# Block attention and two MLPs on one core: Strassen's products for y and o in the last stage too

## The chip, the core and the metric

The kernel runs on one core of a Trainium2 chip. The core has five engines with queues of their own: TensorE (PE, matrix products; PEld is its loading of weights), VectorE (DVE), ScalarE (ACT), GpSimd (POOL) and SyncE (SP), which issues the DMAs. An engine works off its queue in order and waits on semaphores for the others. The metric is the device time of one execution in microseconds (us).

## The reference

```
scores = q @ k.T / 8            # 4 batches, 8 heads, 576 positions, 64 wide
scores[block(i) < block(j)] = -1e9               # blocks of 64 positions
x = softmax(scores) @ v         # -> x: 2304 tokens x 512
x = (sigmoid(x @ w_gate) * (x @ w_val)) @ w_out  # 512 -> 1536 -> 512
h = x @ w_in                                     # 512 -> 2048
out = max(0.01 * h, h) @ w_out2                  # 2048 -> 512
```

The MLP weights arrive as float64, and all is computed to float32's precision.

## The kernel before

Activations are kept transposed, features on partitions, tokens along the free axis. For precision every operand of a product is split into a high and a low half (`hi_lo`: `copy` L336 makes the high half on ACT or DVE, `sub` L350 the low half on DVE, both recorded at L339/L341 and L352), and a product of a 128 x 128 weight block with 512 columns is three matmuls: high x high, high x low, low x high.

The 2304 tokens go through in three stages: 768, 512 and 1024 tokens. In the first, the weights are converted from float64 and their halves are written to HBM (`wd`); later stages load them from there (`weights`, L913; w tiles: 7 buffers of 512 KB). The attention of the next tokens runs between the products of the first two stages. A stage computes gate and val (12 row blocks each, in three groups of four), y = their product times w_out, then h (16 row blocks in four groups) and o. Here y and o are the names of the two output products, and their units carry a group g and an output row block mo. They are delayed by a group (`late`), so that gate or h products stand between a group's making and its use.

In the last stage (b = 2 and 3 are its two halves of 512 tokens) gate, val and h are made in pairs by Strassen's algorithm (Winograd's form): `pair_unit` (L1079) makes two row blocks for both token halves with seven products, B11, T1, T2, B21, T3, B22, T4, six matmuls each (L1099), where eight would be needed. Its results are C11, C12, C21, C22 (`finish`). The sums of weight blocks that it needs were formed in the middle stage by `sums` (L931: additions at L941 on DVE or POOL, then halves, then stores to `ds`), and the sums of x by `mix` (L1032). y and o of the last stage are plain: `half_unit` (L1184), 12 matmuls (L1209) into a PSUM bank of ring mm, and one DVE addition to the accumulator (L1270; xt, shown as x). Their inputs are the four blocks of a group, split by `split_g`.

A planner sets the order. Every operation is given to `Plan.op` with an engine (or two to choose from), a cost, a due time, what it reads and writes, and the ring buffers it uses; `Plan.order` (L149) plays the program through and hands out each engine's next operation, the due time deciding among those that are ready. The due times come from the list `order` (L828 to L850) and the costs.

Of the kernel before, what the change touches and what calls it, by code (L numbers as in the profile page):

```python
# [8 lines left out]
F32 = mybir.dt.float32  # L9
# [9 lines left out]
P = 128  # L19
# [27 lines left out]
def f32(ap):  # L47
    return ap.bitcast(F32)
# [176 lines left out]
def block_attention_then_two_mlps(  # L225
# [35 lines left out]

    const = pool("const", 1)
# [47 lines left out]
    ds = [dram.tile([P, 2, 8 * P], F32, name=f"ds{i}") for i in range((2 * N1 + N2) // 2)]  # L310
# [517 lines left out]
    LATE = [(2, 0), (3, 0), (2, 1), (3, 1), (2, 2), (2, 3), (3, 2), (3, 3)]  # L828
    again = set()
# [3 lines left out]
    for g in range(N1 // G):  # L833
        ms = range(G * g, G * g + G, 2)
        whole([("gate", 2, m) for m in ms])
        rest = late[6:] if g == N1 // G - 1 else []
        whole(late[:len(late) - len(rest)])
        whole([("val", 2, m) for m in ms])
        whole(rest)
        again.update(rest)  # L840
        late = [("y", b, g, mo) for b, mo in LATE]
    whole([("y", b, g, mo) for mos in ((0, 1), (2, 3)) for b in (2, 3) for mo in mos])
    late = []
    for g in range(N2 // G):
        hs = [("h", 2, m) for m in range(G * g, G * g + G, 2)]
        rest = late[6:] if g == N2 // G - 1 else []
        whole(hs[:1] + late[:len(late) - len(rest)] + hs[1:] + rest)
        again.update(rest)
        late = [("o", b, g, mo) for b, mo in LATE]
# [6 lines left out]
    def paired(u):  # L856
        return u[1] == 2 and u[0] in ("gate", "val", "h")
# [70 lines left out]
    def half_pair(u):  # L928
        return {"gate": 0, "val": N1 // 2, "h": N1}[u[0]] + u[2] // 2

    def sums(u, w0, w1):  # L931
# [18 lines left out]
        a11, a12, a21, a22 = [lambda wf=wf, k=k: wf[:, k * q:(k + 1) * q] for wf in wfs for k in range(2)]  # L950
        s1, s2, s3, s4 = [lambda k=k: s[:, k * q:(k + 1) * q] for k in range(4)]
# [8 lines left out]
    def weights_of_pair(u):  # L960
# [7 lines left out]
        load(ws[1], lambda: f32(ws[1][:, :, q:]), wd[k + 1][:, :, q:], P * 8 * q, d - 13, [("wd", k + 1)], [ws[1]])  # L968
# [63 lines left out]
    def mix(d):  # L1032
# [6 lines left out]
        def two(out, x, y, alu, reads, uses, e):  # L1039
            op(  # L1040
                ("dve", "pool"), (c_dve(n), 0.25 + n / 450),
                lambda eng: engines[eng].tensor_tensor(out[:, :n], x(), y(), alu), reads, [out], uses, e, port=True,
            )
# [11 lines left out]
        for k in range(2):  # L1055
            (y1, a1, u1), (y2, a2, u2), (z1, b1, _), (z2, b2, _) = of(k, 2), of(k + 2, 2), of(k, 3), of(k + 2, 3)
            t1, t2, t3, t4 = [r_gf.tile() for _ in range(4)]
            e = d + 2 + 4 * k
            two(t1, z1, y1, ALU.subtract, [*b1, *a1], [t1, *u1], e)
            two(t2, z2, lambda t1=t1: t1[:, :n], ALU.subtract, [t1, *b2], [t1, t2, *u2], e + 0.5)  # L1060
            part("T2", k, lambda t2=t2: t2[:, :n], [t2], [t2], e + 1)
            two(t3, z2, z1, ALU.subtract, [*b1, *b2], [t3, *u1, *u2], e + 1.5)
            part("T3", k, lambda t3=t3: t3[:, :n], [t3], [t3], e + 2)
            two(t4, y2, lambda t2=t2: t2[:, :n], ALU.subtract, [t2, *a2], [t4, t2, *u2], e + 2.5)
            part("T4", k, lambda t4=t4: t4[:, :n], [t4], [t4], e + 3)
            part("T1", k, lambda t1=t1: t1[:, :n], [t1], [t1], e + 3.5)
            part("B21", k, y2, a2, u2, e + 4)
            part("B22", k, z2, b2, u2, e + 4.5)


    places = {"g": [], "sg": [], "tmp": []}
# [6 lines left out]

    def pair_unit(u, ws):  # L1079

# [7 lines left out]
        cost = 6 * c_mm(n)  # L1088
        q = 2 * P
        t = [0.0]  # L1090

        def product(p, first, w, col, x):
            wt = ws[w]
            srcs = [quarter(x, k) for k in range(2)]

            def f():
                for k in range(2):
                    for wl, xl in ((0, 0), (0, 1), (1, 0)):
                        nc.tensor.matmul(  # L1099
                            p[:, :n], lhsT=wt[:, wl, col + k * P:col + (k + 1) * P], rhs=srcs[k][0][:, xl],  # L1100
# [3 lines left out]
            reads = [wt, *[x for _, toks, _ in srcs for x in toks]]  # L1104
            op(
                "pe", cost, f, reads, [p], [p, wt, *[x for _, _, us in srcs for x in us]], d + t[0],
                slack=0.0 if first else CHAIN,
            )
            t[0] += cost
# [7 lines left out]

        out = {}
        for name, b, j in (("C22", 3, 1), ("C11", 2, 0), ("C12", 3, 0), ("C21", 2, 1)):
            if kind == "gate":  # L1120
                gates[b, m + j] = place("sg")
                view, tok, host = gates[b, m + j]
                out[name] = view, tok, host, b, j
            else:
                key = "y" if kind == "val" else "o", b, m + j
                gf[key] = r_gf.tile()
                view, toks, host = held_g[key] = places["g"].pop(0)
                gt[key], g_toks[key] = view, (toks, host)
                f = gf[key]
                out[name] = (lambda f=f: f[:, :n]), (f, 0), f, b, j  # L1130

        def finish(name, p, x=None):
# [12 lines left out]
            if kind == "gate":  # L1145
                op("act", c_act(n, psum), lambda: nc.scalar.activation(dst(), src(), AF.Sigmoid), reads, [tok], uses, e)
                return
            key = "y" if kind == "val" else "o", b, m + j
            if kind == "h":
# [14 lines left out]
            split_g(key, e + 0.6)  # L1164

        a, c, r = b_sc.tile(), b_tp.tile(), b_mm.tile()
# [247 lines left out]
```

## Time and profile before

| | us |
|---|---|
| median of three runs (1007.94 to 1009.1) | 1008.2 |
| the profiled execution | 1007.89 |
| its span on the core | 1006.1 |
| PE busy | 994.5 |
| DVE busy | 645.9 |
| ACT busy | 509.7 |
| POOL busy | 127.3 |

The busy times are shares of one span, and the engines work side by side, so they don't add up. PE's clock was granted in full in every slice (1.00, 2.4 GHz). The page's chain of waits, followed back from the last instruction, is 98% PE.

### The profile page before, as it was taken

The numbers are of one execution on the slowest core, as the hardware profiler recorded it, in microseconds if no ns is written. First come the engines' busy times: TensorE is split into PE (matmuls) and PEld (weight loads), VectorE is DVE, ScalarE is ACT, GpSimd is POOL, SyncE is SP. The second block draws the span as 40 slices with busy tenths as digits, with TensorE's granted clock in tenths as the row PEclk, the third lists the DMA queues.
The fourth block names the chain that finished last, engine by engine and source line by source line (L and its number), as shares of the span: only waits on it lengthen the run. The fifth ranks groups of instructions, "written<-read, shape, count | busy, mean of one in ns | idle before, by whom it ended". The sixth has DMA issues, their size and how long they took to land.

```text
span 1006.1 us, 15306 instructions
## 1 busy us (share of the span) xinstructions
PE 994.5 (99%) x5552; PEld 796.1 (79%) x5552; DVE 645.9 (64%) x1454; ACT 509.7 (51%) x1041; POOL 127.3 (13%) x144
## 2 busy tenths in 40 slices
PE   7999999999999999999999999999999999999998
PEld 4588888978888878777877778788888878888886
DVE  6989989889989657747577665726033357423432
ACT  7988785676766435464455534343333125431420
POOL 2422000220002002211222011102010110000000
PEclk9999999999999999999999999999999999999999
DMA  7488886856876438778767655565446544543542
GB/s 205 143 292 267 274 263 237 257 186 235 280 249 212 167 122 307 262 237 302 229 214 237 226 194 182 184 217 174 150 146 209 156 138 138 165 146 106 177 136 84
DMA packets 75724, 203.91 MB, mean 203 GB/s; under 512 B 8576, under 2 KB 21376, under 8 KB 75648
## 3 DMA queue, kind: packets, MB, share of 16 engines
q1 hardware_dynamic: 75648, 202.93, 62.1%
q8 instruction: 44, 0.72, 0.3%
q14 instruction: 32, 0.26, 0.1%
HBM read 141.56 MB, written 61.34 MB: 202 GB/s over the span
## 4 chain that ended last, share of the span: by engine, by line
PE 98%; DVE 1%; ACT 0%; DMA 0%; issue 0%; SPq 0%
PE mm L1209 63%; PE sc L1099 11%; PE tp L1099 6%; PE sc L425 3%; PE tp L630 3%; PE mm L1099 3%; PE pa L654 2%; PE tp L425 2%; PE tp L566 1%; PE mm L654 1%; PE tp L581 1%; PE pa L425 1%; DMA qk<-in_qk 0%; PE pa L770 0%; PE sc L727 0%; PE mm L581 0%
## 5 line engine op out<-in xcount | busy, mean ns | idle before, releaser
L1209 PE MATMUL mm<-g,w 128*128 128x512 f32 (+1 forms) x1080 | 240.7, 367 | 0.2 <-DVE g L352 0.2
L1209 PE MATMUL mm<-x,w 128*128 128x512 f32 (+2 forms) x1008 | 236.9, 387 | 0.0
L1209 PEld LDWEIGHTS mm<-g,w 128*128 128x128 f32 x1080 | 184.0, 188 | 36.7 <-issue 2.4
L1209 PEld LDWEIGHTS mm<-x,w 128*128 128x128 f32 x1008 | 179.8, 188 | 40.6 <-issue 5.1
L1099 PE MATMUL sc<-both,w 128*128 128x512 f32 x480 | 119.9, 394 | 0.0
L1099 PEld LDWEIGHTS sc<-both,w 128*128 128x128 f32 x480 | 90.3, 188 | 20.6
L497 ACT ACTIVATE both<-both,nm 128x256 f32<-128x256 f32 (+5 forms) x148 | 84.5, 573 | 31.1 <-DVE nm L482 30.1
L893 ACT ACTIVATE mag<-raw 128x512 f32<-128x512 f32 x68 | 45.7, 672 | 47.0 <-DVE wf L907 17.8
L1209 PE MATMUL mm<-sg,w 128*128 128x512 f32 (+1 forms) x288 | 67.4, 365 | 0.0
L352 DVE TENSOR_TENSOR g<-gf,g 128x512 fp32r<-128x512 f32 (+2 forms) x74 | 55.5, 752 | 14.2 <-ACT g L339 14.0
L1270 DVE TENSOR_TENSOR x<-mm,x 128x512 f32<-128x512 f32 x40 | 27.6, 691 | 57.3 <-PE mm L1209 57.2
L907 POOL TENSOR_TENSOR wf<-mag,rnd 128x512 int32<-128x512 int32 x28 | 37.3, 1334 | 206.1 <-DVE w L352 150.2
L1209 PE MATMUL mm<-xa,w 128*128 128x256 f32 x480 | 62.7, 281 | 0.0
L1209 PEld LDWEIGHTS mm<-xa,w 128*128 128x128 f32 x480 | 60.0, 188 | 3.3 <-issue 0.8
L517 POOL TENSOR_SCALAR both<-both,r 128x256 f32<-128x256 f32 (+6 forms) x61 | 36.2, 601 | 183.4 <-DVE r L510 153.8
L1209 PEld LDWEIGHTS mm<-sg,w 128*128 128x128 f32 x288 | 49.9, 188 | 9.4
L482 DVE CUSTOM_DVE_ANT_0 both<-sc,mask 128x256 f32<-128x256 f32 (+6 forms) x101 | 39.3, 424 | 19.4 <-PE sc L425 19.3
L1270 DVE TENSOR_TENSOR acc<-mm,acc 128x512 f32<-128x512 f32 (+1 forms) x60 | 36.0, 600 | 22.9 <-PE mm L1209 22.2
L515 ACT ACTIVATE both<-both,r 128x512 f32<-128x512 f32 (+6 forms) x87 | 45.1, 564 | 8.7 <-DVE r L510 8.6
L901 DVE SCALAR_TENSOR_TENSOR mag<-raw,mag 128x512 int32<-128x512 int32 x68 | 47.5, 700 | 0.3
L425 PE MATMUL sc<-qk 64*128 64x384 f32 (+5 forms) x228 | 42.2, 421 | 5.4 <-DMA qk<-in_qk 5.4
L352 DVE TENSOR_TENSOR w<-wf,w 128x512 fp32r<-128x512 f32 x68 | 46.9, 689 | 0.2
(177 smaller groups left out, 1488.4 us busy)
## 6 DMA issues: line engine op xcount, KB each, us to landing
w<-wd SPq DMA_DIRECT2D x120, 512.0 KB, 4.2
raw<-in_w SPq DMA_DIRECT2D x68, 512.0 KB, 4.4
wd<-w SPq DMA_DIRECT2D x68, 512.0 KB, 4.3
ds<-raw SPq DMA_DIRECT2D x40, 512.0 KB, 5.0
w<-ds SPq DMA_DIRECT2D x40, 512.0 KB, 4.3
qk<-in_qk SPq DMA_DIRECT2D x32, 288.0 KB, 5.0
v<-in_v SPq DMA_DIRECT2D x32, 160.0 KB, 3.1
w<-wd SPq DMA_DIRECT2D x20, 256.0 KB, 3.4
```

Of the source, the lines that this page charges most:

```text
L352: engines[e].tensor_tensor(dst(), a(), f32(b()), ALU.subtract)
L425: nc.tensor.matmul(ps[row:row + nq, col:col + nk], lhsT=tqk[half, 0, q0:q0 + nq], rhs=tqk[half, 1, k0:k0 + nk], start=True, stop=True,)
L482: nc.vector.tensor_tensor_reduce(out=pt[:, n:n + width], in0=ps[:, col:col + width], in1=mask[:, 4 * P + BLK - width:] if masked else mask ...
L497: nc.scalar.activation(pt[:, :n], pt[:, :n], AF.Exp, bias=nm[:, k - 1:k], scale=-1.0, accum_out=sm[:, i:i + 1],)
L515: nc.scalar.activation(pt[:, :n], pt[:, :n], AF.Copy, scale=r[:, i:i + 1])
L517: nc.gpsimd.tensor_scalar(out=pt[:, :n], in0=pt[:, :n], scalar1=r[:, i:i + 1], scalar2=0.0, op0=ALU.mult, op1=ALU.add)
L893: op("act", c_act(n), lambda: nc.scalar.activation(mag[:], words(1).bitcast(F32), AF.Abs), [raw], [mag], [raw, mag], d - 8)
L901: op("dve", c_dve(n), lambda: nc.vector.scalar_tensor_tensor(out=mag[:].bitcast(I32), in0=words(1).bitcast(I32), scalar=-0x40000000, in1=m ...
L907: engines[e].tensor_tensor(wf[:].bitcast(I32), mag[:].bitcast(I32), rnd[:], ALU.add)
L1099: nc.tensor.matmul(p[:, :n], lhsT=wt[:, wl, col + k * P:col + (k + 1) * P], rhs=srcs[k][0][:, xl], start=first and k == 0 and wl + xl == 0 ...
L1209: nc.tensor.matmul(ps[:, :n], lhsT=ws[:, wl, k * P:(k + 1) * P], rhs=srcs[k]()[:, xl, hs], start=k == 0 and wl + xl == 0, stop=k == 3 and ...
L1270: op("dve", c_dve(n), lambda: nc.vector.tensor_tensor(a(), ps[:, :n], a(), ALU.add), [ps], toks_a, [ps, *host], e)
```

## The change

In the last stage y and o become pair units as well: one unit makes two output row blocks (mo, mo + 1) for both token halves from a group's four row blocks, with the same seven products. Their inputs are the group's blocks in Strassen's sums, made by the new `spread` right after val or h (four differences on DVE or POOL, seven splits instead of four). The seven products are added into the four accumulators as each comes (`gather`, DVE). The middle stage forms the sums of weight blocks for y's and o's pairs too (34 pairs instead of 20). On PE each product is now two operations of three matmuls. `mix` makes its parts in another order.

```diff
-    ds = [dram.tile([P, 2, 8 * P], F32, name=f"ds{i}") for i in range((2 * N1 + N2) // 2)]
+    ds = [dram.tile([P, 2, 8 * P], F32, name=f"ds{i}") for i in range(NU // 2)]
...
-    LATE = [(2, 0), (3, 0), (2, 1), (3, 1), (2, 2), (2, 3), (3, 2), (3, 3)]
...
-        whole([("gate", 2, m) for m in ms])
-        rest = late[6:] if g == N1 // G - 1 else []
-        whole(late[:len(late) - len(rest)])
-        whole([("val", 2, m) for m in ms])
...
-    whole([("y", b, g, mo) for mos in ((0, 1), (2, 3)) for b in (2, 3) for mo in mos])
+        whole([("gate", 2, m) for m in ms] + late + [("val", 2, m) for m in ms])
+        late = [("y", 2, g, mo) for mo in (0, 2)]
+    whole(late)
...
+        whole(hs[:1] + late + hs[1:])
+        late = [("o", 2, g, mo) for mo in (0, 2)]
     whole(late)
...
-        return u[1] == 2 and u[0] in ("gate", "val", "h")
+        return u[1] == 2
...
-        load(ws[1], lambda: f32(ws[1][:, :, q:]), wd[k + 1][:, :, q:], P * 8 * q, d - 13, [("wd", k + 1)], [ws[1]])
+        for hl in range(2):
+            load(
+                ws[1], lambda hl=hl: rows_of(u, f32(ws[1][:, hl]), 1), rows_of(u, wd[k + 1][:, hl], 1), P * 4 * q, d - 13,
+                [("wd", k + 1)], [(ws[1], hl)],
+            )
...
+    def spread(kind, m, outs, d):
...
+        def part(name, x):
+            if not places["g"]:
+                return False
+            view, toks, hosts = blocks[kind, g, name, j] = places["g"].pop(0)
+            src, tok, host = outs[x]
+            hi_lo(n, lambda: view()[:, 0], lambda: view()[:, 1], src, [tok], toks[0], toks[1], [host, *hosts], d)
+            return True
+
+        def take(out, x, y):
+            (o, to, ho), (a, ta, ha), (b, tb, hb) = outs[out], outs[x], outs[y]
+            op(
+                ("dve", "pool"), (c_dve(n), 0.25 + n / 450),
+                lambda e: engines[e].tensor_tensor(o(), a(), b(), ALU.subtract), [x for x in (ta, tb) if x is not to], [to],
+                [ho, ha, hb], d, port=True,
+            )
+            return True
...
+        for x in (
+            (part, "B11", "C11"), (take, "C11", "C12", "C11"), (part, "T1", "C11"), (part, "B22", "C22"),
+            (take, "C12", "C22", "C12"), (part, "T3", "C12"), (take, "C22", "C22", "C11"), (part, "T2", "C22"),
+            (part, "B21", "C21"), (take, "C21", "C21", "C22"), (part, "T4", "C21"), (done,),
+        ):
...
+        def gather(name, p):
...
+            if m == 0 and name not in touched:
+                copy(n, dst, lambda: p[:, :n], [p], toks, [p, host], e, True)
+            else:
+                op("dve", c_dve(n), lambda: nc.vector.tensor_tensor(dst(), p[:, :n], dst(), ALU.add), [p], toks, [p, host], e)
...
         product(a, True, 0, 0, "B11")
+        gather("C11", a)
         product(c, True, 2, 0, "T1")
+        gather("C22", c)
+        product(a, False, 2, 1, "T2")
+        gather("C12", a)
+        product(r, True, 0, 1, "B21")
+        gather("C11", r)
         product(a, False, 3, 0, "T3")
+        gather("C22", a)
+        product(c, False, 3, 1, "B22")
+        gather("C12", c)
+        product(a, False, 1, 1, "T4")
+        gather("C21", a)
...
-        if u[1] == 1 and u[0] in ("gate", "val", "h") and u[2] % 2:
-            to_sum.append((u, held[u[0], 1, u[2] - 1], held[u]))
+        if u[1] == 1 and u[-1] % 2:
+            to_sum.append((u, held[*u[:-1], u[-1] - 1], held[u]))
```

How the instructions stand. First PE in the last round of y, before: mm is a half unit's PSUM bank, w a weight tile, and g, qk and acc hold a group's split blocks.

```order
L1209 MATMUL mm_8389<-g_7540,w_8301 128x512 x3
L1209 MATMUL mm_8389<-qk_7620,w_8301 128x512 x3
L1209 MATMUL mm_8389<-acc_7909,w_8301 128x512 x3
L1209 MATMUL mm_8389<-g_7506,w_8301 128x512 x3
L1209 MATMUL mm_8407<-g_7540,w_8329 128x512 x3
L1209 MATMUL mm_8407<-qk_7620,w_8329 128x512 x3
L1209 MATMUL mm_8407<-acc_7909,w_8329 128x512 x3
L1209 MATMUL mm_8407<-g_7506,w_8329 128x512 x3
L1209 MATMUL mm_8423<-g_7504,w_8301 128x512 x4
L1209 MATMUL mm_8423<-g_7506,w_8301 128x512
```

The same round of the changed kernel: sc and tp are the banks of two y units that alternate, and mm with x1 is already h.

```order
L1147 MATMUL tp_8632<-g_7742,w_8575 128x512 x3
L1147 MATMUL sc_8599<-g_7752,w_8575 128x512 x3
L1147 MATMUL sc_8673<-qk_7774,w_8637 128x512 x3
L1147 MATMUL sc_8599<-g_7740,w_8575 128x512 x3
L1147 MATMUL sc_8673<-acc_7830,w_8637 128x512 x3
L1147 MATMUL tp_8660<-g_7706,w_8665 128x512
L1147 MATMUL tp_8660<-g_7740,w_8665 128x512
L1147 MATMUL tp_8660<-g_7706,w_8665 128x512
L1147 MATMUL tp_8660<-g_7742,w_8665 128x512 x3
L1147 MATMUL sc_8599<-acc_7830,w_8613 128x512 x3
L1147 MATMUL mm_8761<-x1_111,w_8719 128x512 x3
L1147 MATMUL sc_8599<-raw_7892,w_8613 128x512 x3
```

Four runs of three on one bank have become runs of three that change banks, and h products now stand between the last y products.

Next DVE in that round, before: L1270 adds a half unit to its accumulator, L352 splits blocks for the last y (g, acc) and for h (both, x1), L1042 is a difference for h.

```order
L352 TENSOR_TENSOR g_7506<-gf_8381,g_7506 128x512
L352 TENSOR_TENSOR acc_7909<-gf_8379,acc_7909 128x512
L1270 TENSOR_TENSOR x0_4987<-mm_8389,x0_4987 128x512
L352 TENSOR_TENSOR both_7145<-x0_4987,both_7145 128x512
L1270 TENSOR_TENSOR x0_5304<-mm_8407,x0_5304 128x512
L352 TENSOR_TENSOR both_7145<-x0_5304,both_7145 128x512
L1270 TENSOR_TENSOR x0_4987<-mm_8423,x0_4987 128x512
L1042 TENSOR_TENSOR gf_8455<-x0_4987 128x512
L352 TENSOR_TENSOR x1_111<-gf_8455,x1_111 128x512
L1270 TENSOR_TENSOR x0_5304<-mm_8439,x0_5304 128x512
L1270 TENSOR_TENSOR x0_5642<-mm_8459,x0_5642 128x512
```

DVE in the same round of the changed kernel: L1219 is `gather`'s addition, L353 the low half of a block, L1100 a difference of `spread`.

```order
L1100 TENSOR_TENSOR gf_7403<-v_7450,gf_7403 128x512
L353 TENSOR_TENSOR g_7752<-v_7453,g_7742 128x512
L1100 TENSOR_TENSOR v_7450<-v_7450,v_7453 128x512
L353 TENSOR_TENSOR g_7740<-gf_7403,g_7740 128x512
L1100 TENSOR_TENSOR gf_7406<-gf_7406,v_7450 128x512
L353 TENSOR_TENSOR acc_7830<-v_7450,acc_7830 128x512
L1219 TENSOR_TENSOR x0_5342<-tp_8632,x0_5342 128x512
L353 TENSOR_TENSOR raw_7892<-gf_7406,raw_7892 128x512
L1219 TENSOR_TENSOR x0_5001<-mm_8639,x0_5001 128x512
L1219 TENSOR_TENSOR x0_5001<-sc_8599,x0_5001 128x512
L1219 TENSOR_TENSOR x0_5687<-sc_8673,x0_5687 128x512
L353 TENSOR_TENSOR both_7339<-x0_5001,both_7339 128x512
```

The differences and splits of the last val pair now stand among the additions of the y units, and there are more of both.

Last SP near the end of the middle stage, before: w from wd is a weight load, ds from raw a store of sums.

```order
L334 DMA ds18_213<-raw_6864 128x1024
L334 DMA ds18_213<-raw_6865 128x1024
L329 DMA w_6932<-wd62_189 128x1024
L329 DMA w_6947<-wd63_190 128x1024
L329 DMA w_6978<-wd50_177 128x1024
L329 DMA w_7005<-wd51_178 128x1024
L329 DMA w_7038<-wd64_191 128x1024
L329 DMA w_7087<-wd65_192 128x1024
L334 DMA ds19_214<-raw_7070 128x1024
```

And of the changed kernel, around the same loads.

```order
L330 DMA w_7107<-wd63_190 128x1024
L330 DMA w_7143<-wd50_177 128x1024
L335 DMA ds24_219<-raw_7132 128x1024
L335 DMA ds24_219<-raw_7133 128x1024
L330 DMA w_7200<-wd51_178 128x1024
L330 DMA w_7216<-wd64_191 128x1024
L335 DMA ds30_225<-raw_7213 128x1024
L335 DMA ds30_225<-raw_7214 128x1024
L330 DMA w_7264<-wd65_192 128x1024
L330 DMA w_7284<-wd66_193 128x1024
L335 DMA ds31_226<-raw_7287 128x1024
L330 DMA w_7316<-wd67_194 128x1024
```

Among the loads of wd50 to wd67 stood the two stores of one pair's sums (ds19, its second one behind the rows shown); now those of three pairs stand there (ds24, ds30, ds31).

## Rows read from the trace of the kernel before

**Rows 1.** Page: each engine's busy us, share of the span, instructions.

```profile
PE 994.5 (99%) x5552; PEld 796.1 (79%) x5552; DVE 645.9 (64%) x1454; ACT 509.7 (51%) x1041; POOL 127.3 (13%) x144
```

**Rows 2.** Waits of PE, whole program: waiter, cause, total us, times, longest us.

```profile
PE sc L425 <- DMA qk<-in_qk: 5.4, 2, 4.9
PE tp L630 <- ACT both L339: 0.8, 1, 0.8
...
PE mm L1209 <- DVE g L352: 0.2, 1, 0.2
```

**Rows 3.** Middle and last stage: us, PE, PEld, DVE, ACT, POOL, clock, DMA, GB/s.

```profile
344.00:653.40 309.40, 308.85 (x1751) 237.15 (x1751) 203.92 (x471) 147.12 (x311) 51.25 (x62) 1.00 0.67 222
653.40:1002.50 349.10, 348.86 (x1507) 282.82 (x1506) 136.69 (x207) 113.92 (x187) 17.66 (x14) 1.00 0.48 154
```

**Rows 4.** Timeline of PE around the last stage's start: start, us, what, count.

```profile
642.54 11.07 PE L1209 MATMUL mm<-g,w 128*128 128x512 f32 x48
653.45 1.56 PE L1099 MATMUL tp<-x,w 128*128 128x512 f32 x6
654.85 1.53 PE L1099 MATMUL sc<-both,w 128*128 128x512 f32 x6
...
664.62 1.53 PE L1099 MATMUL sc<-both,w 128*128 128x512 f32 x6
```

**Rows 5.** Timeline of the end of the program.

```profile
1000.93 0.85 PE L1209 MATMUL mm<-g,w 128*128 128x512 f32 x3
...
1001.62 0.86 PE L1209 MATMUL mm<-sg,w 128*128 128x512 f32 x3
1002.52 0.69 DVE L1270 TENSOR_TENSOR x<-mm,x 128x512 f32<-128x512 f32 x1 [2.09 <-PE mm L1209]
1003.28 0.33 SPq L334 DMA_DIRECT2D out_t<-x  x1
```

**Rows 6.** Three stretches of the middle stage, columns as in rows 3.

```profile
380.00:400.00 20.00, 20.00 (x118) 17.32 (x117) 15.64 (x26) 9.50 (x15) 5.43 (x5) 1.00 0.88 317
400.00:420.00 20.00, 20.00 (x127) 14.68 (x126) 15.09 (x39) 10.91 (x23) 6.10 (x7) 1.00 0.89 290
520.00:540.00 20.00, 20.00 (x127) 14.27 (x126) 18.76 (x47) 9.13 (x24) 7.82 (x9) 1.00 0.69 229
```

**Rows 7.** L941 in the middle stage (DVE, POOL busy); DVE's largest low halves there.

```profile
344.00:653.40 309.40, 44.60 (x89) 32.52 (x31) 1.00 0.67 222
...
L352 DVE TENSOR_TENSOR raw<-raw 128x1024 fp32r<-128x1024 f32 x20 | 24.6, 1231 | 0.7 <-ACT raw L339 0.5
```

**Rows 8.** Waits of DVE in the middle stage: longest total.

```profile
DVE wf L941 <- DMA w<-wd: 26.8, 17, 6.9
```

**Rows 9.** DMA of the middle stage, then of the last: moved; issues, KB, us to landing.

```profile
DMA packets 22074, 68.58 MB, mean 223 GB/s; under 512 B 2400, under 2 KB 4960, under 8 KB 22050
...
DMA packets 24080, 53.82 MB, mean 154 GB/s; under 512 B 1872, under 2 KB 6736, under 8 KB 24062
...
w<-wd SPq DMA_DIRECT2D x50, 512.0 KB, 4.2
w<-ds SPq DMA_DIRECT2D x37, 512.0 KB, 4.3
```

**Rows 10.** Timeline around the last val pairs and the last y before.

```profile
796.56 1.30 POOL L1161 TENSOR_TENSOR gf<-gf,raw 128x512 f32<-128x512 f32 x1 [39.08 <-DVE gf L1139]
797.12 1.29 DVE L1161 TENSOR_TENSOR gf<-gf,raw 128x512 f32<-128x512 f32 x1
...
797.89 1.19 ACT L339 ACTIVATE g<-gf 128x512 fp32r<-128x512 f32 x2 [0.82 <-POOL gf L1161]
798.56 1.29 DVE L352 TENSOR_TENSOR g<-gf,g 128x512 fp32r<-128x512 f32 x2 [0.15 <-ACT g L339]
...
815.10 0.50 PE L1209 MATMUL mm<-g,w 128*128 128x512 f32 x1
...
815.82 1.43 PE L1209 MATMUL mm<-g,w 128*128 128x512 f32 x5 [0.22 <-DVE g L352]
```

**Rows 11.** Two stretches around the last y, columns as in rows 3.

```profile
786.00:803.00 17.00, 17.00 (x76) 13.80 (x75) 6.82 (x11) 4.86 (x8) 2.60 (x2) 1.00 0.57 171
803.00:836.00 33.00, 32.78 (x141) 26.20 (x140) 19.05 (x29) 8.25 (x14) 3.85 (x3) 1.00 0.41 130
```

More of the change, by code (lines that the diff above doesn't have):

```diff
@@ L928, in half_pair, with rows_of @@
     def half_pair(u):
-        return {"gate": 0, "val": N1 // 2, "h": N1}[u[0]] + u[2] // 2
+        return unit(u) // 2
+    def rows_of(u, x, k):
+        if u[0] in ("gate", "val", "h"):
+            return x.rearrange("p (h j c) -> p h j c", h=2, j=2)[:, k]
+        return x.rearrange("p (j h c) -> p j h c", h=2, j=2)[:, :, k]
     def sums(u, w0, w1):
@@ L1077, in place, with done, work @@
         return x
+    def spread(kind, m, outs, d):
+        g, j, n = m // G, m % G // 2, TN
+        def part(name, x):
[13 more added lines that the diff above has]
+            return True
+        def done():
+            places["gf"].extend(outs[x] for x in outs)
+            return True
+        for x in (
[3 more added lines that the diff above has]
+        ):
+            pending.append(x)
+        work()
+    def work():
+        while pending and pending[0][0](*pending[0][1:]):
+            pending.pop(0)
+    pending, blocks = [], {}
     def pair_unit(u, ws):
@@ L1121, in pair_unit @@
                 gates[b, m + j] = place("sg")
[L1122 to L1130, printed above, removed]
+                out[name] = *gates[b, m + j], b, j
+            elif from_x:
+                outs[name] = places["gf"].pop(0)
+                out[name] = *outs[name], b, j
         def finish(name, p, x=None):
@@ new lines, in pair_unit @@
+        product(a, False, 2, 1, "T2")
+        gather("C12", a)
+        product(r, True, 0, 1, "B21")
+        gather("C11", r)
+        product(a, False, 3, 0, "T3")
+        gather("C22", a)
+        product(c, False, 3, 1, "B22")
+        gather("C12", c)
+        product(a, False, 1, 1, "T4")
+        gather("C21", a)
+        if kind == "o" and m == N2 // G - 1:
+            for j in range(2):
+                for b in (2, 3):
+                    stored(b, u[3] + j)
+        if u[3]:
+            for name in BLOCK_NAMES:
+                for j in range(2):
+                    places["g"].append(blocks.pop((kind, m, name, j)))
+            work()
@@ L1202, in half_unit @@
                 uses += g_toks[x][1]
-                if b > 1 and u[3] == 3:
-                    places["g"].append(held_g.pop(x))
         def f():
```

141 lines of the change are left out of this document (78 added, 63 removed).

## The prediction

> **What bounds the kernel now.** I read the busy line first: TensorE (PE) is busy 994.5 of 1006.1 us, the vector engine (DVE) 645.9, ScalarE (ACT) 509.7, GpSimd (POOL) 127.3 [rows 1]. A busy PE could still be a PE that waits with a matmul in flight, so the next view is PE's waits: after 5.4 us for the first load the largest total is 0.8 us, and the only wait in the last stage is 0.2 us [rows 2]. Then the two stretches that the change touches [rows 3]. In the last stage, 653.4 to 1002.5, PE runs 1507 recorded matmuls in 349.1 us, 231.7 ns each, and DVE is busy for 136.69 us of it. In the middle stage, 344 to 653.4, PE is as dense, while DVE is busy for 203.92 of 309.4 us and the DMA engines for 0.67. So a matmul less is about 231.7 ns less, as long as nothing makes PE wait; DVE and the queues have room on average, least in the middle stage. The end is short: after the last matmul one add and one store [rows 5].
>
> **What goes.** By the code, y has 24 half units in the last stage (3 groups, 4 row blocks, 2 column blocks) and o has 32, with 12 matmuls each: 672. In their place stand 6 pair units of y and 8 of o, with 7 products of 6 matmuls: 14 x 42 = 588. 84 matmuls of the same shape go. Do the new ones cost the same? A pair unit in the trace, from its T2 to the next unit's, starts 42 matmuls in 664.62 - 654.85 = 9.77 us, 232.6 ns each [rows 4], against the stage's mean of 231.7 [rows 3]. I take the mean: 84 x 231.7 ns = **19.5 us off**. The bounds of the new matmuls' pace are the pair unit's 232.6 and the 48 half-unit matmuls in 653.45 - 642.54 = 10.91 us, 227.3 each [rows 4]: over 588 matmuls 0.5 us less saved or 2.6 more. The order on PE also cuts each product into two threes; o's half units already change operands every three matmuls, 0.69 us for three (1000.93 to 1001.62 [rows 5]), 230 ns each, so I charge nothing.
>
> **What comes, in the last stage.** Each val and h pair now splits 7 blocks instead of 4 and forms 4 differences: for 14 units 42 copies, 42 subtractions, 56 differences. Each y and o unit adds 7 products into its sums instead of 4: 98 instead of 56, 42 more. On DVE a 512-column pass is 0.69 us alone and 1.29 for two in a row [rows 10]. The order puts 44 differences on DVE and 12 on POOL, so DVE gets 42 + 44 + 42 = 128 passes x 0.65 = 83 us more, 220 of some 334 us. ACT's 42 copies, at 1.19 for two, are 25 us. Neither engine is full, so on average this lies beside PE's work. In most rounds the blocks of a group are used one pair unit or more (9.77 us) after they are started, with gate or h products in between, so I charge nothing there; without that cover each group would cost what the last ones do, below.
>
> Two places have no such cover. After the last val pair come only the last y units and then the mix for h; after the last h pair only the last o units. The chain there: T1 needs C12, which is finished by an add after the sixth product, 1.40 us before the unit's end. Add 0.69, multiply 0.69 (or ACT 0.6), difference 0.69, copy 0.60, subtraction 0.69: 3.3 us, so T1 is there 1.9 us after the unit's end, and PE wants it after one product, at 1.40: 0.5 us late. Later blocks need 1.3 us of DVE each where there is a difference and 0.65 where not, 4 x 1.3 + 3 x 0.65 = 7.2 us against PE's 9.77, so they keep up if DVE does nothing else. Around the last y it does: in 786 to 836 DVE was busy 6.82 + 19.05 = 25.9 of 50 us [rows 11]; the two last val pairs add 14 passes and the y units 6, 20 x 0.65 = 13 us, and the stretch shrinks by 12 matmuls, 2.8 us: 39 of 47, with most of it bunched before and in the y round. Before, PE lost 0.5 us there (a start 0.72 us after the one before, where 0.23 is usual: 815.10 to 815.82 [rows 10]). I take four DVE passes' worth of waits, 2.7 us, for that 0.5: **+2.2**. Bounds: 0 (the order finds other products to run) and 13 (all passes on the path). At the end, the 0.5 of the chain and the wait for one gather before the accumulator is used again: **+1.0**, bounds 0 and 4.
>
> A rule of the Trainium skill bears on the differences that go to POOL. The trace: a POOL multiply of 1.30 us from 796.56 has beside it a DVE one on the same kind of operands that starts at 797.12 and takes 1.29 [rows 10], where 0.69 is usual. The Trainium skill, SBUF — State Buffer, section "SBUF: two separate sides", says that the port pair which the two share is a lock: whoever comes second stands still to the end of the other's instruction. The trace agrees (0.6 us lost). By that rule POOL's passes in the crowded round don't relieve DVE; three of them there would make the +2.2 about +4. The sum stays with +2.2, since most POOL passes lie in rounds with room.
>
> **What comes, in the middle stage.** Sums are now formed for 14 more pairs (6 of w_out's first matrix, 8 of the second), 34 instead of 20. The 20 pairs take 44.60 us of DVE and 32.52 of POOL at L941 [rows 7]; 14 more: 31.2 and 22.8. The low halves, 1231 ns each, add 14 x 1.23 = 17.2 on DVE; the high halves mostly go to ACT. DVE goes from 204 to 252 of 309 us, 82%. PE stood at 20.00 of 20 us with DVE at 18.76 [rows 6], so the load alone is no stall. The stores: 28 of 512 KB, 14.7 MB on 68.58, from 222 to 269 GB/s; PE was full at 317 and 290 [rows 6]. What is new are waits in order: DVE stood 26.8 us, in 17 waits of up to 6.9 us, on weights that had not landed when a sum wanted them [rows 8], and SP's queue holds a store until the sum is made, with the next weight loads behind it. Those 17 waits cost PE nothing that its list shows. I charge **+0.7** for all of it, one wait of a sum's first DVE pass; bounds 0 and 14 x 1.58 (26.8 / 17) = 22.
>
> **Loads of the last stage.** y and o loaded 28 tiles and 4 of them again, 16.8 MB; now 14 units load 3.5 tiles each, 25.7. 53.82 + 8.9 = 62.7 MB in 334 us is 188 GB/s, below the middle stage's 223 [rows 9]. Four tiles of seven belong to one unit, so three of the next can land while it runs: 4.2 to 4.3 us [rows 9] inside 9.77. The fourth is halved into pieces with shorter runs, but it serves the last product alone. Nothing charged; if a load came late it would cost its excess over 9.77 per unit. The end of the program, an add and a store after the last matmul, stays.
>
> **Sum.** -19.5 + 2.2 + 1.0 + 0.7 = -15.6. The profiled execution took 1007.9 us (1.8 around its span); 1007.9 - 15.6 = **992.3 us**. The median of the three runs, 1008.2, is 0.3 higher.
>
> **Rivals.**
> (a) All hidden: the order fills both gaps, even the old 0.5: 1007.9 - 19.5 - 0.5 = 987.9. For it: PE's list of waits is almost empty today. Against: nothing is left to run after the last h pair.
> (b) Every round pays. The accumulator of a y or o unit is used again one product (1.40 us) after its gather may begin; with DVE behind, each of 14 units loses one pass, 14 x 0.65 = 9.1, beside the terms above: 1001.4. For it: gathers can run on DVE alone. Against: DVE at two thirds.
> (c) The middle stage's queues decide and the kernel gets slower: a sum that waits for its weights holds DVE, DVE holds softmax and the store, the store holds SP's next loads, and PE waits for each of the 14 new pairs for the mean of those waits, 1.58 us: 22 for 0.7, 1013.6. It is slower from 1.2 us a pair on ((19.5 - 3.2) / 14). For it: DVE at 82% and more stores in SP's queue. Against: 17 such waits show up nowhere on PE.
> (d) The change doesn't shorten PE's list: excluded by the count of matmuls.
>
> **Chances.** Forecast (989 to 997) 0.58; (a) 0.18; (b) 0.13; (c) 0.06, in milder forms between 1001 and 1008 another 0.05. Range 987.5 to 1000: it holds most of (a) with the pace's bounds, the forecast and half of (b). A difference under 0.2%, 2 us, can't be told from none. Faster 0.93, same 0.02, slower 0.05.
>
> **What would show it.** PE with 84 matmuls fewer and the same 231 to 233 ns between starts in the last stage; no wait before 344 us that is not there today; waits of PE for DVE's subtractions of blocks or for DVE's adds, bunched before the mix for h and at the end, 3 to 5 us together; DVE near 250 us in the middle stage and near 220 in the last. Wrong would be: waits of PE on weight loads, waits spread over all y and o rounds (b), or a middle stage longer than 310 us (c).

## The result, and the profile after

The changed kernel takes 994.8 us (993.8 to 995.4, four runs) against 1008.1 for the kernel before: a ratio of 0.9866, 95% interval 0.9849 to 0.9883, about 13.3 us. The forecast was 992.3 with a range of 987.5 to 1000. The profiled execution took 994.91 us, its span 993.1 (before 1006.1).

First the busy line of the page, against [rows 1]:

```profile
PE 977.9 (98%) x5468; PEld 779.7 (79%) x5468; DVE 779.5 (78%) x1658; ACT 550.3 (55%) x1103; POOL 166.1 (17%) x172
```

5552 - 5468 = 84 matmuls are gone, as counted, and DVE has 133.6 us more work. The two stages follow, with the columns of [rows 3]; the first stretch now ends where o's 48 matmuls do (656.9), the second where the last gather begins (989.4):

```profile
344.00:656.90 312.90, 311.77 (x1760) 238.56 (x1759) 252.45 (x536) 165.99 (x335) 77.82 (x81) 1.00 0.78 262
656.90:989.40 332.50, 329.99 (x1417) 265.22 (x1415) 221.85 (x346) 135.69 (x225) 29.38 (x22) 1.00 0.59 193
```

DVE's 252 and 222 us are the forecast's 252 and 220; DMA's 262 and 193 GB/s its 269 and 188. In both PE is a little less dense than in [rows 3]: 312.90 - 311.77 = 1.1 us and 2.5 us without a matmul, where 0.55 and 0.24 were. The waits of PE say on what (waiter, cause, total us, times, longest us; the first is the start of the program, as in [rows 2]):

```profile
PE sc L426 <- DMA qk<-in_qk: 5.9, 3, 4.6
PE tp L1147 <- DMA w<-ds: 1.1, 1, 1.1
PE tp L631 <- ACT both L340: 0.8, 1, 0.8
PE sc L1147 <- DVE x L1219: 0.8, 1, 0.8
PE tp L1147 <- DVE g L353: 0.8, 1, 0.8
PE tp L1147 <- DVE x L353: 0.8, 1, 0.8
```

Four new waits, one each. The timeline (start, us, what, [idle before <- releaser]) places them at three spots. Its first four lines are the last stage's start, where [rows 4] had o's 48 matmuls directly behind the first six of the pair stage:

```profile
641.87 1.54 PE L1147 MATMUL sc<-both,w 128*128 128x512 f32 x6
644.50 0.94 PE L1147 MATMUL tp<-x,w 128*128 128x512 f32 x3 [1.09 <-DMA w<-ds]
645.28 0.86 PE L1147 MATMUL sc<-both,w 128*128 128x512 f32 x3
645.98 11.07 PE L1299 MATMUL mm<-g,w 128*128 128x512 f32 x48
...
813.38 1.68 POOL L1100 TENSOR_TENSOR v<-gf,v 128x512 f32<-128x512 f32 x1 [1.23 <-DVE qk L353]
813.95 0.94 PE L1147 MATMUL tp<-raw,w 128*128 128x512 f32 x3 [0.77 <-DVE g L353]
...
836.69 0.68 DVE L353 TENSOR_TENSOR x<-gf,x 128x512 fp32r<-128x512 f32 x1
...
837.42 1.44 PE L1147 MATMUL tp<-x,w 128*128 128x512 f32 x5 [0.76 <-DVE x L353]
...
987.72 0.98 PE L1147 MATMUL sc<-g,w 128*128 128x512 f32 x3 [0.79 <-DVE x L1219]
988.54 0.86 PE L1147 MATMUL sc<-qk,w 128*128 128x512 f32 x3
989.43 0.69 DVE L1219 TENSOR_TENSOR x<-sc,x 128x512 f32<-128x512 f32 x1 [1.76 <-PE sc L1147]
```

644.50 is the start; 813.95 and 837.42 lie in the last y round, the first by this list behind a split of the last val pair's block (a load lands there too, see below), the second behind one of the mix for h; 987.72 is the end, where the last T4 product writes the PSUM buffer that C22's gather still reads.

To size them I take the time from one recorded matmul's start to the next in the last stage, less the usual 0.232 us, and add up what is over 0.1 us. For comparing profiled spans I count from the first MLP matmul (56.28 us in before, 56.43 after) to the end, because the attention ahead of it varies by 2 us between the profiled executions (the first MLP matmul starts at 55.5 to 57.6). All kernels of this study so read (us; leave-out kernels are marked *):

```
kernel     ratio to before [95%]      from first MLP matmul   gaps: start   last y   end
before     1                          949.79                        0.0     0.72    0.0
after      0.9866 [0.9849, 0.9883]    936.64                        1.26    3.49    1.05
y_only     0.9965 [0.9951, 0.9978]    946.15                        1.14    3.24    0.0
o_only     0.9926 [0.9913, 0.9938]    941.72                        1.58    0.11    1.05
old_sums*  0.9861 [0.9847, 0.9874]    936.12                        1.14    3.23    1.05
take_dve   0.9878 [0.9865, 0.9892]    937.74                        1.08    5.05    1.04
act_load   0.9870 [0.9855, 0.9885]    937.30                        3.26    3.30    1.04
no_diff*   0.9864 [0.9849, 0.9878]    935.76                        0.94    3.16    1.15
add_dve    0.9873 [0.9858, 0.9887]    937.14                        1.67    3.25    1.05
end_bank   0.9874 [0.9857, 0.9891]    935.92                        1.05    3.22    0.0
t1_after   0.9856 [0.9842, 0.9871]    935.86                        1.58    3.25    1.15
t1_end     0.9857 [0.9841, 0.9874]    934.92                        1.88    3.20    0.0
no_diff2*  0.9835 [0.9821, 0.9850]    934.21                        1.38    0.76    1.05
sums_t1*   0.9840 [0.9827, 0.9853]    934.06                        0.28    3.22    1.04
```

The intervals are about 1.5 us to either side, so differences of about 1 us between two changed kernels are read from the gaps, one execution each; the ratios only bear them out where they are 2 us or more. The spans have a spread too: from the first MLP matmul to the last stage's first product the kernels whose edits all lie behind that product take 584.5 to 585.8 us (before: 584.9), so 1 us of span alone shows nothing.

### The profile page after: what moved, and what is told of

Its sections match the earlier page's. It is cut to its first block, busy times and chain, and to the rows that moved or that the text cites. A ratio compares the mean times of both kernels' runs of the same rounds, so it can differ in the third digit from the quotient of the medians.

```text
span 993.1 us, 15675 instructions
## 1 busy us (share of the span) xinstructions
PE 977.9 (98%) x5468; PEld 779.7 (79%) x5468; DVE 779.5 (78%) x1658; ACT 550.3 (55%) x1103; POOL 166.1 (17%) x172
## 4 chain that ended last, share of the span: by engine, by line
PE 94%; DVE 3%; DMA 1%; ACT 1%; SPq 0%; issue 0%; POOL 0%; DVEq 0%; ACTq 0%
PE mm L1299 48%; PE sc L1147 17%; PE tp L1147 9%; PE mm L1147 4%; PE tp L631 3%; PE sc L426 3%; PE pa L655 2%; PE tp L426 2%; PE tp L567 1%; DMA qk<-in_qk 1%; PE mm L655 1%; PE tp L582 1%; DMA w<-ds 1%; DVE x L1219 0%; SPq L330 0%; DVE g L353 0%
## 5 line engine op out<-in xcount | busy, mean ns | idle before, releaser
L1299 PE MATMUL mm<-g,w 128*128 128x512 f32 (+1 forms) x792 | 164.0, 358 | 0.0
L1299 PEld LDWEIGHTS mm<-g,w 128*128 128x128 f32 x792 | 130.0, 189 | 23.4 <-issue 2.3
L1147 PE MATMUL sc<-both,w 128*128 128x512 f32 x480 | 130.6, 396 | 0.1
L1299 PE MATMUL mm<-xa,w 128*128 128x256 f32 x480 | 62.7, 281 | 0.0
L353 DVE TENSOR_TENSOR g<-gf,g 128x512 fp32r<-128x512 f32 (+2 forms) x73 | 57.8, 793 | 3.5 <-ACT g L340 3.4
L340 ACT ACTIVATE g<-gf 128x512 fp32r<-128x512 f32 (+2 forms) x61 | 40.0, 657 | 23.6 <-DVE gf L1330 11.9
L516 ACT ACTIVATE both<-both,r 128x384 f32<-128x384 f32 (+6 forms) x94 | 48.6, 566 | 6.9 <-DVE r L511 6.9
L1219 DVE TENSOR_TENSOR x<-sc,x 128x512 f32<-128x512 f32 x44 | 30.2, 689 | 23.2 <-PE sc L1147 23.2
L1299 PE MATMUL mm<-sg,w 128*128 128x512 f32 (+1 forms) x216 | 47.4, 355 | 0.0
L353 DVE TENSOR_TENSOR w<-wf,w 128x512 fp32r<-128x512 f32 x68 | 46.5, 684 | 0.2
```

The source lines that it names most:

```text
L340: nc.scalar.activation(dst(), src(), AF.Copy)
L353: engines[e].tensor_tensor(dst(), a(), f32(b()), ALU.subtract)
L516: nc.scalar.activation(pt[:, :n], pt[:, :n], AF.Copy, scale=r[:, i:i + 1])
L1147: nc.tensor.matmul(p[:, :n], lhsT=wt[:, wl, at * P:(at + 1) * P], rhs=view[:, xl], start=first and k == 0 and wl + xl == 0, stop=k == 1 an ...
L1299: nc.tensor.matmul(ps[:, :n], lhsT=ws[:, wl, k * P:(k + 1) * P], rhs=srcs[k]()[:, xl, hs], start=k == 0 and wl + xl == 0, stop=k == 3 and ...
```

## Experiments

**The two halves alone.** In y_only and o_only one of the two stays in half units, and its sums are not formed.

```
     def paired(u):
-        return u[1] == 2
+        return u[1] == 2 and (u[0] in ("gate", "val", "h") or u[0] == STRASSEN)    # "y", or "o"
...
-        if u[1] == 1 and u[-1] % 2:
+        if u[1] == 1 and u[-1] % 2 and (u[0] in ("gate", "val", "h") or u[0] == STRASSEN):
```

> Only y goes by Strassen's algorithm in the last stage, o stays as it was. Theory (every matmul that goes gives 231.7 ns, and the change loses time at four places only): 36 matmuls fewer, -8.3 us; the last y round pays its 2.8 us; 6 new pairs of sums instead of 14, early in the middle stage, 0.3; the late load at the last stage's start is gone with o's sums, 0; pace 0.2: 5.0 us under the kernel before, about 1003.1. Rival 1 (the loss of 6.5 us lies in the 14 new pairs of sums, 0.46 us each, and the y round is an accident of the order): -8.3 + 6 x 0.46 = -5.5, but with a last y round without waits. Rival 2 (every y and o round pays a pass of VectorE): -8.3 + 6 x 0.65 = -4.4, with the waits spread over all y rounds.

> Only o goes by Strassen's algorithm in the last stage, y stays as it was. Theory: 48 matmuls fewer, -11.1 us; the end +1.0; the late load of sums at the last stage's start +1.3, since the o sums are the late ones; middle stage +0.4; the last y round nothing more than before; pace 0.2: 8.2 us under the kernel before, about 999.9. With y_only the two gains should add up to the 13.3 us of the whole change. Rival 1 (0.46 us for each pair of sums): -11.1 + 1.0 + 8 x 0.46 = -6.4, about 1001.7. Rival 2 (a pass of VectorE for each o round): -11.1 + 8 x 0.65 = -5.9, about 1002.2.

Measured: 1004.0 against 1008.2 (ratio: 3.5 us, 2.2 to 4.9) and 1000.4 (7.5 us, 6.3 to 8.8). By the table's spans 3.6 and 8.1, 11.7 together, where the whole change has 13.15. The y and end columns came out as the theory has them: y pays at the last y round alone, o at the end alone, and no round between pays anything, against rival 2. But y_only still waits 1.14 us at the start, without any of o's sums, so the theory's reason for that wait is wrong; and since each half pays a start that the whole pays once (1.26), the gains fall short of the whole's by about that.

**Without the new sums.** old_sums leaves out the forming; the loads stay.

```
     def half_pair(u):
-        return unit(u) // 2
+        return unit(u) // 2 - {"y": N1, "o": N2 // 2}.get(u[0], 0)
...
-        if u[1] == 1 and u[-1] % 2:
+        if u[1] == 1 and u[-1] % 2 and u[0] in ("gate", "val", "h"):
```

> The 14 new pairs' sums and their stores are left out of the middle stage; y and o load the sums of the h and gate/val pairs in their place, so the loads and the products of the last stage stay, with other values. Theory: the new sums cost 0.7 us in the middle stage and 1.3 us through the stores that stand ahead of the first loads of sums on SP's queue: 2.0 us under the changed kernel, about 992.8, and the wait for the load at the last stage's start is gone. Rival 1 (the sums carry the whole loss of 6.5 us): about 988.3. Rival 2 (they are hidden, and the wait at the start has another cause, the loads themselves): 994.8, with the wait still there.

Measured: 994.0, and 0.5 us off the span: rival 2 by the time. The start waits about as long as with the sums (1.14 for 1.26 us), but not, as the rival has it, for the load: it waits behind VectorE's split of T1:

```profile
643.63 0.47 PE L1147 MATMUL tp<-x,w 128*128 128x512 f32 x1
644.73 0.73 PE L1147 MATMUL tp<-x,w 128*128 128x512 f32 x2 [0.64 <-DVE x L353]
```

The sums' line L939 (us, DVE, POOL, clock, DMA, GB/s) is then little burden, though it grew in the changed kernel as forecast, by 31 us on DVE and 26 on POOL against [rows 7]:

```profile
344.00:656.90 312.90, 75.58 (x143) 58.60 (x57) 1.00 0.78 262
```

By themselves the sums and their stores cost half a microsecond of the span or less, which is inside its spread. The load of sums that the profile named was only the last of several inputs to come.

**The load from another queue.**

```
+        queue = "act" if u[0] == "gate" and u[2] < 4 else "sp"
         load(ws[2], lambda: f32(ws[2][:]), ds[i][:, :, :2 * q], ..., [ws[2]], queue)
         load(ws[3], lambda: f32(ws[3][:]), ds[i][:, :, 2 * q:], ..., [ws[3]], queue)
```

> The loads of sums for the first two gate pairs of the last stage are issued from ScalarE's queue, not from SP's, where they stand behind stores that wait for the last o pairs' sums. Theory: the wait of 1.26 us at the last stage's start (644.50) is of SP's order; it goes, or most of it: about 993.5, 1.3 us under the changed kernel; the sums themselves stay. Rival (the load is late because the DMA engines are full there, or ScalarE has the same order): the wait stays, 994.8 or more.

Measured: 995.3; nothing won. The order on PE changed with it (o's 48 matmuls first again), and the wait came back behind them, twice, behind VectorE:

```profile
659.62 0.96 PE L1148 MATMUL sc<-both,w 128*128 128x512 f32 x3 [1.28 <-DVE wf L342]
665.47 0.97 PE L1148 MATMUL sc<-both,w 128*128 128x512 f32 x3 [1.46 <-DVE sg L1181]
```

**The order at the start.** A new theory: six matmuls of the pair stage's second and third product (T1 and T2) are put ahead of o's 48 before their inputs are there.

```
+                    if u == ("gate", 2, 0) and x != "B11":
+                        toks = [*toks, ("o_done",)]
...
+        if u == ("o", 1, N2 // G - 1, 3) and last:
+            writes.append(("o_done",))
```

> The first gate pair's products other than those with B11 stand behind the 48 products of the last o units of the middle stage, as in the kernel before; nothing else changes. New theory: the 1.26 us at the last stage's start come from these six products (T1 and T2) being put ahead of o's 48, where neither their sums nor their mixed factors have come yet, and not from the new sums (without the new sums the wait was still there, behind VectorE): the wait goes, 1.0 to 1.3 us under the changed kernel, about 993.6 by its 994.8. Rival (the inputs of the pair stage are late as such): the wait comes again behind o's products, and the time stays.

Measured: 994.6, the rival's answer: the wait at 644 is gone, and two others stand behind the 48.

```profile
659.58 0.97 PE L1149 MATMUL tp<-xa,w 128*128 128x512 f32 x3 [0.27 <-ACT wf L340]
...
666.86 2.34 PE L1149 MATMUL sc<-both,w 128*128 128x512 f32 x9 [0.79 <-DVE sg L1182]
```

Neither the sums nor the order alone, then. What both have in common is VectorE: the last o pairs' sums and the mix of x fall into the same 25 us. The last kernel takes both away (the edits of old_sums and of t1_after together).

> Two edits together: the 14 new pairs' sums are left out (y and o load the sums of other pairs, so values differ, loads and products stay), and the first gate pair's products other than those with B11 stand behind o's 48. Each alone left a wait of 1.1 to 1.4 us of PE between 643 and 668 us. Theory: the start of the last stage is late since VectorE has the last o pairs' sums and the mix of x at once there (21.6 of 25 us busy from 640 to 665, 17.0 before), and the order of PE only chooses which product waits: without both, no wait over 0.2 us is left between 640 and 670, 1.2 us under the changed kernel, about 993.5, and VectorE's busy time from 640 to 665 is back near 17 to 19 us. Rival (the pair stage's inputs are late for the new reads of weights, which stay here): 0.8 us or more of waits stay.

Measured: 992.7, ratio 0.9840, 2.6 us under the changed kernel by the spans, and no wait over 0.2 us at the start. That is more than the 1.2 of the theory: 1.0 is the start's gaps, 0.5 an earlier first product (inside the spread), 0.3 the last y round, and 0.8 stands in no gap and stays unexplained. The stretch 640 to 665 (us, PE, PEld, DVE, ACT, POOL, clock, DMA, GB/s), and behind it 810 to 842 where it is used below, kernel by kernel; before:

```profile
640.00:665.00 25.00, 25.00 (x110) 20.45 (x109) 17.01 (x27) 11.81 (x19) 2.94 (x2) 1.00 0.63 205
810.00:842.00 32.00, 31.78 (x137) 25.32 (x136) 22.15 (x34) 11.80 (x20) 2.88 (x3) 1.00 0.36 116
```

after:

```profile
640.00:665.00 25.00, 23.91 (x104) 19.27 (x103) 21.64 (x34) 11.63 (x18) 5.29 (x3) 1.00 0.78 263
810.00:842.00 32.00, 30.28 (x125) 22.33 (x124) 30.38 (x49) 13.90 (x23) 7.17 (x5) 1.00 0.50 158
```

old_sums:

```profile
640.00:665.00 25.00, 24.36 (x105) 19.44 (x104) 17.82 (x27) 11.66 (x20) 5.76 (x2) 1.00 0.60 194
```

t1_after:

```profile
640.00:665.00 25.00, 24.73 (x109) 19.94 (x108) 20.92 (x35) 13.27 (x20) 5.60 (x3) 1.00 0.79 272
```

sums_t1:

```profile
640.00:665.00 25.00, 24.98 (x110) 20.16 (x109) 17.72 (x27) 11.79 (x19) 5.75 (x2) 1.00 0.61 200
```

Only sums_t1 has PE at 24.98 of 25, as before the change. With VectorE free but these six matmuls early (old_sums), they wait for their splits; with the six late but VectorE at 20.92 (t1_after), the pair stage waits for its own adds. The wait needs two causes to be removed. That the sums act here through VectorE's time, and not through the stores that go with them, is read from the releasers; no run parts the two.

**The last y round.** take_dve makes GpSimd's share of `spread`'s differences on VectorE; no_diff leaves out the last val pair's differences; no_diff2 those and the eight of the mix for h. A pair has four differences, not the eight that the two expectations count: 52 of 56 are left in no_diff's trace, so no_diff2 leaves out twelve passes, not sixteen.

```
# take_dve
-                ("dve", "pool"), (c_dve(n), 0.25 + n / 450),
+                "dve", c_dve(n),
# no_diff and no_diff2: in spread
-            pending.append(x)
+            if x[0] is not take or (kind, m) != ("y", N1 - 2):
+                pending.append(x)
# no_diff2: in mix, second time (for h)
+            else:
+                t1, t2, t3, t4 = z1, z2, z2, y2
```

> The differences between C11 to C22 that give the second factors of y and o are all made by VectorE (0.65 us each) and none by GpSimd (1.68 us each). Theory: in the last y round VectorE is busy without a gap, so what GpSimd made there comes on top of it: the wait behind GpSimd's 1.68 us goes, and a few VectorE passes come: between 1 us faster and 1.5 us slower than the changed kernel, 994.8 +- 1.5, and nothing elsewhere. Rival (GpSimd is what makes the round late: its passes hold the port that both use): 2 us or more faster, about 992.8.

> The last val pair's eight differences are left out (y's last products take undiffered factors, so the values are others; matmuls, splits and sums stay). Theory: the last y round is late since VectorE has more work there than 28 us hold; eight passes of 0.65 us less (or some of 1.68 us on GpSimd) give back most of the 2.8 us: about 992.5. Rival (the round is late for the order of the splits, or for the h factors behind it): under 0.5 us, about 994.5.

> The last val pair's eight differences are left out, and the eight of the mix of y's result for h as well (other values in y's last products and in all of h's; matmuls, splits and sums stay). Theory 1 (VectorE has more work between 796 and 842 us than fits): sixteen passes less, the waits of PE between 810 and 838 us fall from 3.5 to under 1 us, 2.5 us under the changed kernel, about 992.3. Theory 2 (the round is late for the length of the chain: last gather, split, product, which no difference lengthens by more than a pass): the waits stay at 2 us or more, as without the val differences alone (3.2), 994 or more.

Measured: take_dve 996.1, 1.1 us longer in the span, with 5.05 us of gaps in the round for 3.49. So GpSimd's two differences there don't hold the round up; the order was planned anew with them on VectorE, and 0.55 of the 5.05 is a wait for a load of weights (810.90). no_diff 994.4: the gaps fall by 0.33 only, which is its rival. no_diff2 992.5, 2.4 us shorter, gaps 0.76: theory 1. The two fit together once one sees where no_diff waits. In the round's first half, up to 824, its gaps fall from 1.8 to 0.7 us; in the second, at 830 to 834 behind a gather and the mix's splits, they grow from 1.7 to 2.4. Most of the round is one line of VectorE work from the last val pair to h's first products; four passes less in its first half only bring PE sooner to the second. In no_diff2 one wait is left:

```profile
815.00 0.94 PE L1153 MATMUL tp<-raw,w 128*128 128x512 f32 x3 [0.48 <-DVE qk L353]
```

This wait, 0.6 to 0.9 us of gaps, stands in eleven kernels (813.95 in the changed one), and in eight of them the profile names a load of sums and not VectorE. The chain of old_sums (start, us, what), then what the changed kernel's SyncE waited for before it issued that load at 809.59 (total us, times, longest):

```profile
809.59 0.02 issue
809.60 3.98 DMA w<-ds
813.58 0.14 issue
813.71 0.93 PE tp L1147 x3
```

```profile
SPq L330 <- PE tp L1147: 2.3, 1, 2.3
```

In all eleven the product starts 0.13 to 0.14 us after that load has landed, in no_diff2 too, where it is issued at 810.93 and lands at 814.87; the split that the profile names there ends at 815.00, with the product's start, while a product that follows VectorE starts about 0.04 us after it. In the changed kernel load and split come within 0.1 us of each other (813.82 and 813.91). So one wait of the round, about 0.65 us, is a load's: SyncE could issue it only when PE had finished with a weight tile of the last val pair, and it took 3.9 to 4.2 us to land. No run took it away.

VectorE's busy time from 810 to 842 doesn't tell what the twelve passes were worth, since what comes later moves in; PE's does (no_diff2):

```profile
810.00:842.00 32.00, 31.52 (x136) 25.05 (x136) 30.15 (x52) 11.62 (x20) 1.30 (x1) 1.00 0.53 172
```

136 matmuls started where the changed kernel starts 125 and the one before 137.

**More VectorE work in the middle rounds.**

```
+            if name in ("C12", "C21") and m < (N1 if kind == "y" else N2) // G - 1:
+                op("dve", c_dve(n), lambda: nc.vector.tensor_tensor(dst(), dst(), dst(), ALU.max), [], toks, [host], e + 0.1, port=True)
```

> One more VectorE pass (max of a sum with itself, which changes no value) behind three of the seven gathers of each y and o unit, in all rounds but the last of y and the last of o: 30 passes of about 0.65 us, 19.5 us of VectorE time. Theory: VectorE works 222 of the 332 us of the last stage and no product waits for it in the middle rounds, so it costs nothing: 994.8, at most 995.8. Rival (each gather is on the path of the products, so that each round pays what VectorE does more): 10 units x 1.3 to 2.0 us, 1008 to 1014; at one pass in the path for each unit, 1001.

Measured: 995.6, span from the first MLP matmul 0.5 longer, and 0.41 of that is at the start. VectorE worked 19 us more at no cost that shows (the last stage of add_dve, against 221.85 above):

```profile
656.90:989.40 332.50, 330.25 (x1418) 265.37 (x1416) 240.82 (x374) 136.29 (x226) 30.73 (x23) 1.00 0.57 193
```

**The end.**

```
+        last = kind == "o" and m == N2 // G - 1 and u[3]
+        if last:
+            gather("C21", a)
         product(c, False, 3, 1, "B22")
         gather("C12", c)
-        product(a, False, 1, 1, "T4")
-        gather("C21", a)
+        more = b_mm.tile() if last else a
+        product(more, bool(last), 1, 1, "T4")
+        gather("C21", more)
```

> In the last o unit the product with T4 goes to a PSUM buffer of its own, and C21 gathers twice (one pass more), so that T4's product need not wait until C22's gather has read the buffer. Theory: the wait of 0.94 us at 987.72 goes, the chain's last step stays one gather: 0.9 us under the changed kernel, about 993.9. Rival (VectorE decides the end: the extra pass stands in the line of gathers): 0 to 0.7 us slower, 994.8 to 995.5.

> The first gate pair's products behind o's 48, and in the last o unit T4's product in a PSUM buffer of its own. Theory: both waits go, 1.2 + 1.05 us: 2.2 us under the changed kernel, about 992.6, with the waits of the last y round (3.5 us by the gaps over 0.1 us) as the only ones left. Rival (they hide each other or come back later): 993.5 or more.

Measured: 995.1 (993.3 to 997.4, too wide to tell) and 993.9. In both traces the gap at the end is 0, and the last product isn't late (end_bank, PE and then VectorE):

```profile
985.49 0.84 PE L1147 MATMUL sc<-g,w 128*128 128x512 f32 x3
986.17 0.84 PE L1147 MATMUL mm<-qk,w 128*128 128x512 f32 x3
```

```profile
986.37 1.29 DVE L1219 TENSOR_TENSOR x<-sc,x 128x512 f32<-128x512 f32 x2 [1.35 <-PE sc L1147]
987.76 0.69 DVE L1219 TENSOR_TENSOR x<-mm,x 128x512 f32<-128x512 f32 x1
```

But the extra gather (the second of the x2) is not free. The last product ends at 986.17 + 0.84 = 987.01, and the last gather starts only at 987.76, when the extra one is through; in the changed kernel it starts 0.03 us behind the product (989.43 against 988.54 + 0.86). So about 0.7 of the 1.05 us comes back behind the product, by the rival's mechanism. The chain of end_bank's end runs through VectorE:

```profile
986.37 1.30 DVE x L1219 x2
...
987.76 0.69 DVE x L1219
```

The span is 0.7 us shorter for end_bank, some 0.4 of it at the end, and 1.7 for t1_end, the shortest of the kernels that compute everything; but 0.9 of the 1.7 lies ahead of the last stage, where nothing was edited, and its ratio can't be told from the change's (0.9857 and 0.9866). t1_end's 2.2 us did not come, since the start's wait only moved and the extra gather took back most of the end's.

## Why the prediction was right, and which terms were off

The sum was -19.5 + 2.2 + 1.0 + 0.7 = -15.6; the span shows -13.0. Term by term:

- **84 matmuls, -19.5: held.** The count is exact. The gaps taken out, the last stage's pace is 231.6 ns for 231.3, about 0.4 us over its matmuls.
- **The end, +1.0: held** at 1.05, for one of its two reasons: the gather that must read a PSUM buffer before the next product writes it. In end_bank, with a buffer more, this wait of PE is gone.
- **The last y round, +2.2: 3.49 - 0.72 = 2.8.** VectorE's queue is shown by no_diff2 to be most of it, but the line of work runs on through the mix for h, where I had counted it only up to y's last product, and about 0.65 us of the gaps is a load's. That four passes' worth of waits came so near is in part luck.
- **The middle stage, +0.7, with the last stage's start in nothing: the step that failed most.** The pair stage's first product (six matmuls) starts 0.7 us later than before (641.87; before it had this row), or 0.55 counted from the first MLP matmul:

```profile
641.17 1.53 PE L1099 MATMUL sc<-both,w 128*128 128x512 f32 x6
```

  That is as much as the 0.7, but it shows little: the spread above is 584.5 to 585.8 us, and old_sums, without the new sums, has 585.4 like the changed kernel. The 1.26 behind it was in no term. I took VectorE's mean over each stage (82% and two thirds) and looked for local crowding only at the last y and at the end; the third place where two lots of work meet, the last o pairs' sums and the mix of x at the seam of the stages, I didn't look at, though the rule was the same. There too the order on PE, which I had read, puts six matmuls (T1 and T2) between the first product and o's 48; I costed them as matmuls moved and not as matmuls that wait. In sums_t1, without both causes, the start's gaps are 1.0 us less (0.28 for 1.26).
- **Rival (b), each round pays: absent.** No gap over 0.1 us in the middle rounds, and 30 more passes there are free. **Rival (c): absent**, and VectorE's waits for weights, 26.8 us in 17 [rows 8], fell by half, where (c) had them grow (the middle stage after):

```profile
DVE wf L939 <- DMA w<-wd: 12.8, 12, 2.3
```

- **Loads, nothing charged: the amount held, the price did not.** The last stage moves 64.04 MB for the 62.7 forecast:

```profile
DMA packets 37308, 64.04 MB, mean 193 GB/s; under 512 B 2816, under 2 KB 14848, under 8 KB 37289
```

  But I let three tiles of the next unit land while one runs, at 4.2 to 4.3 us inside 9.77. In the last y round two units alternate, and a load of sums was issued only at 809.59, when PE released a tile: PE stood 0.94 us until it had landed (with VectorE's split as late), 0.6 to 0.7 in the ten others. "Waits of PE on weight loads" was one of my signs of being wrong, and here it came. At the start too a load was the last input by little; there other inputs are as late without it (old_sums, t1_after).

- **The skill's lock rule.** A GpSimd pass in the changed kernel has a VectorE split of 1.54 us beside it, where 0.68 is usual:

```profile
831.89 1.31 POOL L1045 TENSOR_TENSOR gf<-x 128x512 f32<-128x512 f32 x1
832.22 1.54 DVE L353 TENSOR_TENSOR both<-x,both 128x512 fp32r<-128x512 f32 x1
```

  The Trainium skill, SBUF — State Buffer, section "SBUF: two separate sides", has whichever of the two starts first hold the port pair for its whole instruction, and by it the +2.2 was to be +4. The stall shows, but the price doesn't: it was +2.8, and with the differences moved from GpSimd to VectorE 4.3 (5.05 - 0.72).

In all: -19.5 of matmuls, +0.7 and +1.26 at the seam, +2.8, +1.05, 0.4 of pace: -13.3, for the -13.0 of the span.

Not settled: why the six matmuls of T1 and T2 go ahead of o's 48. T1's split is earlier in the changed mix, which would explain it, but that edit wasn't undone alone.

## What to carry to other kernels

A busy share over a stage prices nothing: 30 further VectorE passes were free in the rounds with cover, and leaving out twelve gave 2.4 us where val, y and h follow each other. So list every seam at which one stage's late work and the next one's first work fall on the same engine, and price each of them. And when the profile names one releaser of a wait, take that one away before believing it: here the load, the sums and the order were each changed alone, and each time another input was as late. It helps to look at the same wait in the traces of all variants: the one in the last y round was put down to VectorE in three and to a load in eight, and only its distance from the landing was the same in all.

## What the runs showed of the hardware that I had not expected

GpSimd's differences of 1.3 to 1.7 us, some of which lengthen a VectorE pass beside them, were still worth having: with them on VectorE, at 0.68 us each, the span was 1.1 us longer. Loads and stores at 262 GB/s mean in the middle stage, for 222 before, delayed no product there.
